# A two-layer mixture-of-experts behind a Fourier transform: where the second expert's token search stands in the program

## The chip, the cores and the metric

The kernel runs on one core of a Trainium2 chip. The metric is the device time of one execution in microseconds (us), smaller is better. Before the change it is 1285.11 us, the median of three runs (1282.51 to 1293.55).

A core has a matrix engine (TensorE, PE in the profile; the loads of its stationary operands are shown apart as PEld), a vector engine (VectorE, DVE), an activation engine (ScalarE, ACT), a general engine (GpSimd, POOL) and an engine that here only issues transfers (SyncE, SP). Each works through its own list of instructions in order and waits on semaphores for the others.

## What is computed

The input is transformed by the real part of a two-dimensional Fourier transform; its 9984 rows go through a first mixture-of-experts in which every expert takes exactly as many rows as its share, in the order of the logits, and the result goes through a second one with a plain arg-max.

```
X = fft(fft(x, axis=1), axis=2).real            # (4, 2496, 256) -> 9984 rows of 256

# first mixture: 8 experts, each takes cap = 9984 / 8 = 1248 rows
order = argsort(-(x @ w_gate).flatten())
for idx in order:                                # greedy, best logit first
    tok, e = idx // 8, idx % 8
    if assigned[tok] >= 0 or counts[e] >= cap: continue
    assigned[tok] = e; counts[e] += 1
for e in range(8):
    out[assigned == e] = relu(x[assigned == e] @ w1[e]) @ w2[e]

# second mixture, on the first one's output: e = argmax(x @ w_gate2),
# each row times its softmax weight and a sigmoid gate
```

## The kernel before

The program has three parts. `Fft` (to about 150 us of the span) does the transform with matrix products against tables (L305); its last loop, `rows` (L361), builds rows of the transformed input on VectorE, ScalarE and GpSimd and writes them to a buffer in memory (`xd<-xr`, L387). `Moe1` (to about 800 us) is the first mixture, `Moe2` the second.

The greedy assignment is not done row by row. `Select` (L443) runs eight *phases*. In each, the next expert to become full, and its 1248 rows, are found by a search for a threshold: eight *rounds* and a last count. A round is a loop between two engines: VectorE compares all logits with eight thresholds (L516), TensorE counts (ten small products, L521), VectorE folds the counts (L525 to L533), TensorE sums over the partitions (one product, L538; in the first phase L540), VectorE picks the new lower bound (L568, L573). Ahead of the rounds a phase prepares on VectorE (L548 to L562): the best logit of every row, which expert it belongs to, the steps of the search. Behind the last count it names the expert (`s_ei`, L598), takes its column out of the logits (L630) and numbers the chosen rows (to L633). I number phases, lists and experts from 0.

`places(k)` (L635) turns the numbers into a *list* of row indices: on VectorE L639 to L649 build one-hot factors `ha` and `hb`, TensorE multiplies them (four groups of ten products, L663, a `yield wait` ahead of the first), a second product (L673) and VectorE (L678 to L681) give `s_idx`. With the list GpSimd gathers the rows from `xd` (ten indirect transfers, L850).

`Moe1.ffn(k)` (L969) is the dense work of expert k in three chunks of rows: TensorE transposes the gathered rows (L867), ScalarE and VectorE split them in a high and a low half (L869, L870), TensorE makes the hidden layer (48 products a chunk, L801), ScalarE, VectorE and GpSimd split that (L881 to L887; the GpSimd share goes through three `hf` buffers that ScalarE writes, L884), and ten blocks of 24 products (L809) give the output, evacuated by ScalarE (L898). `route` (L901) then does the second mixture's gate for the expert's rows: some twenty small VectorE operations (L908 to L957), eleven products (L928, L930), two writes (L947, L948) and ten indirect scatters on GpSimd (L962). While the first expert waits for its rows, products on the weights that have already arrived keep TensorE at work (`busy`, L1011).

What stands where in the engines' lists is decided twice. `Flow` (L1115) holds a modelled clock: a unit of dense work moves it on by its length, and side generators (search, `prepare`, weights, gates, route, keep2) are advanced whenever their due time has come; what a generator yields is a delay, or a condition. Where the dense work cannot go on, `until` (L1160) advances the side work alone. The tile framework's scheduler then orders each engine's instructions out of what was emitted.

Before the change `Select.run` (L466) goes straight on from phase 0 and list 0 to phase 1, held only by `placed >= k - AHEAD`, which is true at once for k = 1. `Moe1.run` (L1083) starts the dense work of expert k when `ready >= k`, that is when list k, its gather, its first transposition and its weights have been emitted (`prepare`, L1018).

## Time and profile before

| | |
|---|---|
| runs | 1285.11, 1293.55, 1282.51 us |
| the profiled execution: its own time | 1291.67 us |
| its span, first to last instruction | 1289.9 us |
| TensorE busy | 1165.5 us, 90% of the span |
| VectorE / ScalarE / GpSimd busy | 57% / 35% / 39% |
| TensorE clock granted, mean share of full speed | 0.960 |

The profile's page gives busy times and the chain that ended last; the trace behind it can be asked for the instructions of a stretch in order of time. A row of that timeline has the start in us, the duration in us, engine, line, operation, the tile written and the tiles read, the shapes, how many were merged (x10), and in brackets how long the engine stood idle before it and what ended that. A group "x10" of TensorE is timed from its first start to its last end. A granted clock of 1.00 is 2.4 GHz, 0.50 is 1.2 GHz.

### The profile page before, as it was taken

How to read it: one execution, taken by the hardware profiler on the slowest of the kernel's cores; microseconds unless marked ns; L12 is line 12 of the kernel's file. 1: busy time of each engine (PE TensorE's matmuls, PEld its weight loads, DVE VectorE, ACT ScalarE, POOL GpSimd, SP SyncE). 2: the span in 40 equal slices, each digit the busy share in tenths (PEclk: the TensorE clock that was granted, in tenths of full speed). 3: DMA queues.
4: the chain of work that ended last, by engine and by line, in shares of the span. 5: the costliest groups of instructions: out<-in, count | busy, mean ns of one | idle time of the engine just before them, and what ended most of it. 6: DMA issues, size and time to landing. Idle time of an engine off the chain costs nothing. (4 is left out here: it accounts for less than half of the span.)

```text
span 1289.9 us, 25053 instructions
## 1 busy us (share of the span) xinstructions
PE 1165.5 (90%) x9998; PEld 837.6 (65%) x9998; DVE 733.8 (57%) x1885; ACT 447.7 (35%) x960; POOL 506.4 (39%) x495
## 2 busy tenths in 40 slices
PE   7999789878979969889896999799999999989998
PEld 4654456655646637557583756467576799878887
DVE  5867869784858857886562574443433333333333
ACT  3422344353523723535352443122322222222221
POOL 4723343475372660531505034524332333333321
PEclk8999789999899979999997999899999999999999
DMA  7835513131230651574846458443534266678782
GB/s 272 329 108 187 180 54 111 61 106 41 99 81 34 157 136 50 109 251 137 245 138 166 144 155 294 121 167 119 177 111 168 103 239 240 238 287 299 271 322 97
DMA packets 80040, 212.95 MB, mean 165 GB/s; under 512 B 11851, under 2 KB 48987, under 8 KB 69169
## 3 DMA queue, kind: packets, MB, share of 16 engines
q1 hardware_dynamic: 65360, 180.42, 41.9%
q0 software_dynamic: 14560, 30.91, 8.0%
q8 instruction: 79, 1.29, 0.4%
q14 instruction: 41, 0.33, 0.1%
HBM read 162.17 MB, written 50.42 MB: 165 GB/s over the span
## 5 line engine op out<-in xcount | busy, mean ns | idle before, releaser
L809 PEld LDWEIGHTS <-ht 128*128 128x128 f16 (+1 forms) x3912 | 383.5, 100 | 100.7 <-issue 26.2
L809 PE MATMUL py<-wh,ht 128*128 128x272 f16 (+2 forms) x3264 | 407.4, 281 | 25.4 <-issue 14.8
L801 PE MATMUL ph<-xt,wh 128*128 128x384 f16 (+4 forms) x2352 | 392.3, 318 | 7.2 <-DVE ht L887 4.0
L801 PEld LDWEIGHTS <-wh 128*128 128x128 f16 x2352 | 212.2, 100 | 128.6 <-issue 18.6
L1340 ACT ACTIVATE ht<-ph 128x512 f16<-128x512 f32 x166 | 97.9, 597 | 339.8 <-PE ph L801 269.3
L1341 DVE SCALAR_TENSOR_TENSOR ht<-ph,ht 128x512 f16<-128x512 f32 x166 | 113.7, 690 | 132.5 <-ACT ht L1340 118.7
L962 POOL DMA_INDIRECT lst<-r_en,r_pi x80 | 83.9, 1049 | 167.6 <-DVE r_pi L956 98.1
L881 ACT ACTIVATE ht<-ph 128x384 f16<-128x384 f32 (+1 forms) x192 | 98.4, 515 | 104.5 <-PE ph L801 89.3
L1353 POOL DMA_INDIRECT out<-ot,tarow x54 | 54.4, 1007 | 167.5 <-DVE ot L1352 156.4
L887 DVE SCALAR_TENSOR_TENSOR ht<-ph,ht 128x384 f16<-128x384 f32 (+1 forms) x147 | 85.0, 583 | 24.1 <-ACT ht L881 20.6
L850 POOL DMA_INDIRECT xg<-xd,s_idx x80 | 83.6, 1045 | 33.1 <-issue 23.2
L898 ACT ACTIVATE yr<-py 128x272 f32<-128x272 f32 x80 | 31.6, 395 | 173.1 <-PE py L809 121.3
L885 POOL TENSOR_TENSOR ht<-hf,ht 128x384 f16<-128x384 f32 (+1 forms) x45 | 48.3, 1076 | 88.9 <-ACT hf L884 82.1
L305 PE MATMUL big<-y,tab 128*128 128x36 f16 (+3 forms) x660 | 80.8, 274 | 1.2 <-DVE y L256 1.2
L809 PE MATMUL py<-wp,ht 128*128 128x256 f16 x648 | 75.9, 276 | 5.2 <-ACT ht L1340 3.9
L801 PE MATMUL ph<-xt,wp 128*128 128x256 f16 (+2 forms) x624 | 75.1, 279 | 3.8 <-DVE ht L1341 2.4
L1353 POOL DMA_INDIRECT out<-ot,tbrow x29 | 28.9, 995 | 116.1 <-DVE ot L1352 108.5
L1352 DVE TENSOR_SCALAR ot<-py,g 128x256 f32<-128x256 f32 x45 | 21.7, 483 | 83.9 <-PE py L809 71.5
L801 PEld LDWEIGHTS <-wp 128*128 128x128 f16 x624 | 51.5, 98 | 25.0 <-issue 7.7
L1077 DVE SCALAR_TENSOR_TENSOR wp<-g,wp 128x1024 f16<-128x1024 f32 x32 | 39.1, 1227 | 42.9 <-ACT wp L1076 33.3
L305 PEld LDWEIGHTS <-tab 128*128 128x128 f16 x660 | 38.7, 97 | 29.9 <-issue 2.7
L1352 DVE TENSOR_SCALAR ot<-py,xg 128x256 f32<-128x256 f32 x38 | 18.3, 483 | 64.7 <-PE py L809 57.1
(250 smaller groups left out, 1398.7 us busy)
## 6 DMA issues: line engine op xcount, KB each, us to landing
wh<-wsd SPq DMA_DIRECT2D x50, 1024.0 KB
wp<-wsd SPq DMA_DIRECT2D x26, 1024.0 KB
wf<-moe_w SPq DMA_DIRECT2D x32, 512.0 KB
g<-moe_w SPq DMA_DIRECT2D x32, 512.0 KB
wsd<-wp SPq DMA_DIRECT2D x32, 512.0 KB
xa<-xa SPq DMA_DIRECT2D x8, 1280.0 KB
xd<-xr SPq DMA_DIRECT2D x20, 512.0 KB
yd<-yr SPq DMA_DIRECT2D x8, 1156.5 KB
```

The source lines that it names most:

```text
L305: self.nc.tensor.matmul(dst, self.tabs[par][k][:, cs, c, u], self.y[par][:, cs, w, c, bs, qs], start=(n == 0), stop=(n == 3 * NCH - 1))
L801: Flow.pe = nc.tensor.matmul(dst, w1[:, dk, a, fk * 128:fk * 128 + 128], xt[:, b, dk, :n], start=(k == 0), stop=(k == 5))
L809: Flow.pe = nc.tensor.matmul(dst, ht[:, a, fk, t0:t0 + m], w2[:, fk // 4, b, fk % 4], start=(fk == 0 and a == 0 and b == 0), stop=(fk == 7 ...
L850: nc.gpsimd.indirect_dma_start(out=xg[:m, t], out_offset=None, in_=self.xd, in_offset=bass.IndirectOffsetOnAxis(ap=idx[:m, t:t + 1], axis=0))
L881: self.act = nc.scalar.activation(ht[:, 0, fk, :n], ph[:, :n], AF.Relu)
L885: nc.gpsimd.tensor_sub(ht[:, 1, fk, :n], hf[:, :n], ht[:, 0, fk, :n])
L887: nc.vector.scalar_tensor_tensor(ht[:, 1, fk, :n], ph[:, :n], 0.0, ht[:, 0, fk, :n], op0=OP.max, op1=OP.subtract)
L962: s = nc.gpsimd.indirect_dma_start(out=ent, in_=en[:m, t], in_offset=None, out_offset=bass.IndirectOffsetOnAxis(ap=pi[:m, t:t + 1], axis=0))
L1340: nc.scalar.activation(hi, src, AF.Relu)
L1341: nc.vector.scalar_tensor_tensor(lo, src, 0.0, hi, op0=OP.max, op1=OP.subtract)
L1352: nc.vector.tensor_scalar(ot, py[:, :D], g[:, h, D:D + 1], 2.0 ** -10, op0=OP.mult, op1=OP.mult)
L1353: st = nc.gpsimd.indirect_dma_start(out=self.out, in_=ot, in_offset=None, out_offset=bass.IndirectOffsetOnAxis(ap=row[:, 1, u + h:u + h + ...
```

## The change

Four edits. (1) `Select.run` waits ahead of phase 1 until `begun` is set; `Moe1.run` sets it at the point where the first expert's dense work begins to be emitted. (2) The preparation of phase 1 on VectorE (L548 to L562) is tied behind the last VectorE operation of list 0 (L681) by `issue_after`. (3) The modelled delay ahead of the first matrix products of list 0 becomes 7.0 instead of 6.0; the lists of the other experts keep 6.0. (4) The reduction that writes a list is kept under a name, for (2). What is computed stays the same.

```diff
@@ -394,6 +394,7 @@
 AHEAD = 3
+FIRST = 7.0
@@ -462,17 +463,24 @@
         self.placed = self.chosen = -1
+        self.begun = False
 
     def run(self):
 
         yield from self.start()
         for k in range(8):
             yield lambda: self.placed >= k - AHEAD
+            if k == 1:
+                yield lambda: self.begun
             yield from self.phase(k)
...
+    def behind(self, k):
+
+        return self.tc.issue_after(self.listed.ins) if k == 1 else ExitStack()
@@ -544,23 +552,24 @@
     def phase(self, k):
...
-        vm = w.tile([128, 80], F32, name="vm")
-        nc.vector.tensor_reduce(vm, self.lm, axis=AX.X, op=OP.max)
...
+        with self.behind(k):
+            vm = w.tile([128, 80], F32, name="vm")
+            nc.vector.tensor_reduce(vm, self.lm, axis=AX.X, op=OP.max)
...
@@ -647,7 +656,7 @@
-        wait = 6.0
+        wait = 6.0 if k else FIRST
@@ -678,7 +687,7 @@
-            nc.vector.tensor_reduce(self.idx[k], nf.rearrange("p g t -> p t g"), axis=AX.X, op=OP.add)
+            self.listed = nc.vector.tensor_reduce(self.idx[k], nf.rearrange("p g t -> p t g"), axis=AX.X, op=OP.add)
@@ -1108,6 +1117,7 @@
             flow.until(lambda: self.ready >= k and self.routed >= k - 2)
             self.at = k
+            self.sel.begun = True
             self.ffn(k, flow)
```

Line numbers rise by up to ten in the changed file: L548 there is L557, L639 is L648, L521 is L529, L538 is L546, L801 is L810, L809 is L818, L850 is L859, L867 is L876, L885 is L894, L928 and L930 are L937 and L939, L962 is L971.

Three places of the built program, as each engine's list has them. First VectorE at list 0, before; `vm`, `oe`, `ax`, `s_oh` belong to the preparation of phase 1, `u`, `pos`, `pi` to the list:

```order
L630 TENSOR_TENSOR lm<-lm,pen 128x640
L548 TENSOR_REDUCE vm<-lm 128x80
L553 TENSOR_TENSOR oe<-lm,vm 128x640
L613 CAST ct<-px 80x2
L554 TENSOR_TENSOR oe<-oe,s_w_94 128x640
L556 TENSOR_REDUCE ax<-oe 128x80
L621 SCALAR_TENSOR_TENSOR u<-px,gm,mm_1788 128x80
L622 TENSOR_TENSOR u<-px,mm_1788 128x80
L557 TENSOR_TENSOR s_oh<-s_w_94,ax 128x640
L623 TENSOR_TENSOR u<-u 128x80
```

The same place now:

```order
L639 TENSOR_TENSOR lm<-lm,pen 128x640
L622 CAST ct<-px 80x2
L630 SCALAR_TENSOR_TENSOR u<-px,gm,mm_1788 128x80
L631 TENSOR_TENSOR u<-px,mm_1788 128x80
L632 TENSOR_TENSOR u<-u 128x80
L634 SCALAR_TENSOR_TENSOR u<-u,mm_1788 128x80
L636 SCALAR_TENSOR_TENSOR s_alive<-u,s_alive 128x80
L640 TENSOR_SCALAR u<-u 128x80
L642 TENSOR_TENSOR pos<-u 128x80
L648 CAST pi<-pos 128x80
L353 SCALAR_TENSOR_TENSOR xg_1866<-big,xf 128x512
L649 TENSOR_SCALAR pi<-pi 128x80
```

The preparation of phase 1 and its first comparison (L516) have left this stretch; they stand behind the list (from L690, formerly L681), among the last rows of the transform and the first weights. On TensorE the first ten products of the list stand behind 35 products of the transform of 384 columns instead of 42.

Second, TensorE where expert 0 ends and expert 1 begins, before. The last rows of L809 are expert 0's last output block, L801 is expert 1's first hidden product; expert 1's first transpositions (L867) stand some blocks earlier:

```order
L809 MATMUL py<-wh,ht 96x272
L538 LDWEIGHTS ch
L538 MATMUL sp<-rd,ch 128x16
L786 LDWEIGHTS wt
...
L801 LDWEIGHTS wh
L801 MATMUL ph<-xt,wh 128x384
```

Now (L818 is the last block, L529 and L546 are rounds of phase 2, L937 and L939 the eleven products of expert 0's route, L876 the first transpositions of expert 1):

```order
L818 MATMUL py<-wh,ht 96x272
L546 LDWEIGHTS ch
L546 MATMUL sp<-rd,ch 128x64
L529 LDWEIGHTS s_oh
...
L937 MATMUL pt<-r_o_3405,ch 128x80
...
L939 MATMUL pt<-r_o_3405,ch 128x88
L546 LDWEIGHTS ch
L546 MATMUL sp<-rd,ch 128x64
L529 LDWEIGHTS s_oh
...
L876 MATMUL pt<-cf,xg 128x128 x3
L546 LDWEIGHTS ch
L546 MATMUL sp<-rd,ch 128x64
L810 LDWEIGHTS wh
L810 MATMUL ph<-xt,wh 128x384
```

Between the last output product of expert 0 and the first hidden product of expert 1 there now stand two and a half rounds of phase 2, expert 0's route and expert 1's first transpositions, and no dense work. The last product of list 1 (L673) is followed by only 38 output products of expert 0.

Third, GpSimd from expert 0's last hidden rows to expert 1's first, before:

```order
L885 TENSOR_TENSOR ht<-hf,ht 128x480 x2
L777 TENSOR_TENSOR wt<-wf,wt 128x256
L850 DMA xg<-xd,s_idx_85 128x256 x7
L885 TENSOR_TENSOR ht<-hf,ht 128x480
L850 DMA xg<-xd,s_idx_85 128x256 x2
L850 DMA xg<-xd,s_idx_85 96x256
L777 TENSOR_TENSOR wt<-wf,wt 128x256 x5
L885 TENSOR_TENSOR ht<-hf,ht 128x384 x2
```

And now:

```order
L894 TENSOR_TENSOR ht<-hf,ht 128x480 x3
L786 TENSOR_TENSOR wt<-wf,wt 128x256
L859 DMA xg<-xd,s_idx_85 128x256 x9
L859 DMA xg<-xd,s_idx_85 96x256
L786 TENSOR_TENSOR wt<-wf,wt 128x256
L971 DMA lst<-r_en,r_pi 81920x2 x10
L894 TENSOR_TENSOR ht<-hf,ht 128x384
```

Expert 0's ten scatters now stand in one piece ahead of the first hidden rows of expert 1, where they were spread among them and behind them.

## Rows read from the trace of the kernel before

**Rows 1.** The page, busy time of the engines: us (share of the span), instructions.

```profile
PE 1165.5 (90%) x9998; PEld 837.6 (65%) x9998; DVE 733.8 (57%) x1885; ACT 447.7 (35%) x960; POOL 506.4 (39%) x495
```

**Rows 2.** Table by stretch; the first line names the columns after the stretch.

```profile
core 0: us, PE busy (x) PEld busy (x) DVE busy (x) ACT busy (x) POOL busy (x), PEclk, DMA share, GB/s
...
137.70:145.20 7.50, 7.50 (x53) 5.31 (x53) 3.15 (x5) 0.00 (x0) 0.00 (x0) 0.54 0.57 188
...
249.60:275.00 25.40, 17.99 (x157) 11.62 (x157) 25.18 (x74) 17.34 (x43) 13.84 (x14) 1.00 0.33 110
```

**Rows 3.** Timeline of TensorE at list 0.

```profile
125.62 8.12 PE L305 MATMUL big<-y,tab 128*128 128x512 f16 x47
...
137.68 1.02 PE L663 MATMUL px<-ha,hb 128*128 128x40 f16 x10 [3.94 <-DVE ha L649]
...
140.00 3.06 PE L305 MATMUL big<-y,tab 128*128 128x384 f16 x9
```

**Rows 4.** Timeline of VectorE ahead of list 0's products.

```profile
123.67 0.82 DVE L548 TENSOR_REDUCE vm<-lm 128x80 f32<-128x640 f32 x1
124.53 0.82 DVE L553 TENSOR_TENSOR oe<-lm,vm 128x640 f16<-128x640 f32 x1
...
125.38 0.49 DVE L554 TENSOR_TENSOR oe<-oe,s_w 128x640 f16<-128x640 f16 x1
125.91 0.82 DVE L556 TENSOR_REDUCE ax<-oe 128x80 f16<-128x640 f16 x1
...
127.00 0.81 DVE L557 TENSOR_TENSOR s_oh<-s_w,ax 128x640 f16<-128x640 f16 x1
...
130.09 0.81 DVE L558 TENSOR_TENSOR s_vv<-vm,s_alive 128x80 f32<-128x80 f32 x1
...
131.51 1.34 DVE L516 SCALAR_TENSOR_TENSOR s_msk<-s_vv,s_lo,s_jw 128x640 f16<-128x640 f32 x1
...
134.09 0.76 DVE L641 TENSOR_SCALAR pi<-pi 128x80 int32<-128x80 int32 x1
134.78 0.19 DVE L643 CAST pa<-pi 128x80 f16<-128x80 int32 x1
```

**Rows 5.** Timeline of GpSimd: the last of eight additions of the transform's rows there.

```profile
134.08 0.71 POOL L378 TENSOR_TENSOR xr<-xg,xg 128x256 f32<-128x256 f32 x1
```

**Rows 6.** Timeline of GpSimd, then TensorE: first gather and first product of expert 0.

```profile
159.45 1.47 POOL L850 DMA_INDIRECT xg<-xd,s_idx  x1 [3.74 <-DMA xd<-xr]
...
165.74 0.33 PE L867 MATMUL pt<-cf,xg 128*128 128x128 f32 x1 [0.55 <-DMA xg<-xd,s_idx]
167.40 0.32 PE L801 MATMUL ph<-xt,wh 128*128 128x384 f16 x1 [1.33 <-ACT xt L869]
```

**Rows 7.** Timeline of TensorE, expert 0's first chunk: a round of phase 1.

```profile
174.88 0.20 PE L538 MATMUL sp<-rd,ch 64*128 64x64 f16 x1 [1.68 <-DVE rd L533]
```

**Rows 8.** Timeline: list 1's products, its first gather, last block of expert 0.

```profile
209.76 1.02 PE L663 MATMUL px<-ha,hb 128*128 128x40 f16 x10
...
220.44 0.96 POOL L850 DMA_INDIRECT xg<-xd,s_idx  x1 [4.53 <-DVE zs L573]
...
247.93 1.59 PE L809 MATMUL py<-wh,ht 128*96 128x272 f16 x12
...
249.88 2.44 PE L801 MATMUL ph<-xt,wh 128*128 128x384 f16 x14
```

**Rows 9.** Timeline: a round of phase 2 on TensorE, one operation of expert 0's route.

```profile
239.97 0.50 PE L521 MATMUL sp<-s_msk,s_oh 128*64 128x64 f16 x10
...
241.35 0.20 PE L538 MATMUL sp<-rd,ch 64*128 64x64 f16 x1
...
243.50 0.50 PE L521 MATMUL sp<-s_msk,s_oh 128*64 128x64 f16 x10
...
249.99 0.23 DVE L908 TENSOR_REDUCE r_mx<-yr 128x10 f32<-128x80 f32 x1
```

**Rows 10.** The page, costliest groups: busy us, mean ns of one, idle before.

```profile
L962 POOL DMA_INDIRECT lst<-r_en,r_pi x80 | 83.9, 1049 | 167.6 <-DVE r_pi L956 98.1
```

More of the change, by code (lines that the diff above doesn't have):

```diff
@@ L546, in phase @@
         f, h = self.f, self.h
-        vm = w.tile([128, 80], F32, name="vm")
-        nc.vector.tensor_reduce(vm, self.lm, axis=AX.X, op=OP.max)
-        sh = [128, 80, 8]
-        wt = self.w16[:, None, :].to_broadcast(sh)
-        oe = w.tile(sh, F16, name="oe", bufs=1)
-        nc.vector.tensor_tensor(oe, self.lm, vm[:, :, None].to_broadcast(sh), op=OP.is_equal)
-        nc.vector.tensor_mul(oe, oe, wt)
-        ax = w.tile([128, 80], F16, name="ax")
-        nc.vector.tensor_reduce(ax, oe, axis=AX.X, op=OP.max)
-        nc.vector.tensor_tensor(self.oh, wt, ax[:, :, None].to_broadcast(sh), op=OP.is_equal)
-        nc.vector.tensor_add(self.vv, vm, self.alive)
-        wd = w.tile([128, 1], F32, name="wd")
-        nc.vector.tensor_sub(wd, self.hi, self.lo0)
-        nc.vector.tensor_scalar(self.wr, f["pw"], wd, None, op0=OP.mult)
-        nc.vector.tensor_mul(self.jw, f["jt"][:, None, :].to_broadcast([128, ROUNDS, T]),
-                             self.wr[:, :, None].to_broadcast([128, ROUNDS, T]))
+        with self.behind(k):
+            vm = w.tile([128, 80], F32, name="vm")
+            nc.vector.tensor_reduce(vm, self.lm, axis=AX.X, op=OP.max)
+            sh = [128, 80, 8]
+            wt = self.w16[:, None, :].to_broadcast(sh)
+            oe = w.tile(sh, F16, name="oe", bufs=1)
+            nc.vector.tensor_tensor(oe, self.lm, vm[:, :, None].to_broadcast(sh), op=OP.is_equal)
+            nc.vector.tensor_mul(oe, oe, wt)
+            ax = w.tile([128, 80], F16, name="ax")
+            nc.vector.tensor_reduce(ax, oe, axis=AX.X, op=OP.max)
+            nc.vector.tensor_tensor(self.oh, wt, ax[:, :, None].to_broadcast(sh), op=OP.is_equal)
+            nc.vector.tensor_add(self.vv, vm, self.alive)
+            wd = w.tile([128, 1], F32, name="wd")
+            nc.vector.tensor_sub(wd, self.hi, self.lo0)
+            nc.vector.tensor_scalar(self.wr, f["pw"], wd, None, op0=OP.mult)
+            nc.vector.tensor_mul(self.jw, f["jt"][:, None, :].to_broadcast([128, ROUNDS, T]),
+                                 self.wr[:, :, None].to_broadcast([128, ROUNDS, T]))
         lo = self.lo0
```

## The prediction

> **What bounds the kernel now.** I read the page first: TensorE is busy for 1165.5 us of the span, 90% [rows 1]. So a change gains only where it takes away time in which TensorE stands still or runs at its low clock, and it loses where it makes such time. I therefore looked in the timeline for TensorE's idle times in the part that the change touches, from the end of the transform to the end of expert 1.
>
> Three things are to be seen. First, at list 0: TensorE ends its products of the transform at 133.74 (125.62 + 8.12) and then stands for 3.94 us until VectorE has `ha` for the list [rows 3]. VectorE is late because it does phase 1's preparation in between: seven operations of that phase stand ahead of or among those of the list, 0.82 + 0.82 + 0.49 + 0.82 + 0.81 + 0.81 + 1.34 = 5.91 us [rows 4]. The idle time has an aftermath: in the 7.5 us behind it the granted clock is 0.54, close to the lower level of 1.2 GHz [rows 2]. Second, the gather of expert 0 does not wait for the list. Its first transfer waits for the last write of the transform's rows, and starts at 159.45; the first product of expert 0 comes at 167.40, 7.95 us later [rows 6]. So list 0 matters only as it delays TensorE's way through the end of the transform, which ends in those writes. Third, between expert 0 and expert 1 nothing is waited for: the last block starts at 247.93 and runs 1.59, the first product of expert 1 follows at 249.88, and its gather had begun at 220.44, 29 us ahead [rows 8]. That lead is what the change spends.
>
> **The change, part by part.**
>
> *List 0 earlier (edits 2 and 3).* The 5.91 us leave VectorE's path to the list, so `ha` is no longer what TensorE waits 3.94 us for, or not for so long. The bounds: TensorE now comes to the list seven products sooner (35 instead of 42 of them ahead), at 8.12 / 47 = 0.17 us each 1.2 us sooner [rows 3], and VectorE up to 5.9 us sooner, so that the wait could vanish. But VectorE's small operations now meet GpSimd's eight additions, which end at 134.79 [rows 5]: beside them a small operation takes 0.76, without them 0.19 [rows 4]. Four of them (L640 to L644) at 0.57 more is 2.3 us of the 5.9 given back, which leaves 3.94 + 1.2 - 3.6 = 1.5 us of wait. I take that end, since the additions are where they were: 2.4 us are gained; the range is 0 to 3.9.
>
> *The clock behind it.* About 16 products of the transform in that stretch go at 3.06 / 9 = 0.34 instead of 0.17 us [rows 3]: 2.7 us. The list's own products lose nothing: ten take 1.02 at the low clock and 1.02 at the full one [rows 3, 8]. I take 2.5 us gained, because I expect that 1.5 us of idle time leave the clock up; if not, 0. The Trainium skill (TensorE: Matmul & The Clock Gate, Terms) counts the penalty as the low-clock time times the share of pulses left out. By that it would be 7.5 x 0.46 = 3.4 us, and the sum below 0.9 lower; no run here settles between the two yet, and I keep the rows' number.
>
> Together TensorE is at the end of the transform, the last writes out, the gather begun and expert 0 started 4.9 us earlier. The work that follows the transform's last products (its rows on VectorE) is as long as before: the preparation and three counts change places there.
>
> *Phase 1 inside expert 0 (edit 1).* All eight rounds of phase 1 now lie in expert 0; three of them lay ahead. They are moved, not added: phase by phase the same products are done. In the first chunk the wait of 1.68 us for a round [rows 7] goes, since the first round now stands behind 24 products. List 1 comes late in expert 0, tightly behind the phase; I allow 0.7 us for new waits there (0 to 2). Expert 0: -1.0.
>
> *The border of experts 0 and 1.* Phase 1 is three rounds later against the dense work, and so are list 1 and its gather. Only 38 output products follow the last product of list 1; at 1.59 / 12 = 0.13 us they last 5.0 us [rows 8]. The gather needs 7.95 us from its first transfer to the first product [rows 6], so at least 3 us are left bare. What decides, though, is TensorE's own list, which is in order: two and a half rounds of phase 2 stand ahead of expert 1's first transposition and product, with nothing to fill them. From counts to sum (L521 to L538) a round takes 1.38 us, from there to the next counts 2.15 [rows 9]. From the last output product: 0.9 (the rest of a round whose counts start just before it) + 2.15 + 1.38 + 2.15, then the counts' 0.43, and from the transposition to the first product 1.66 [rows 6]: 8.7 us. Expert 0's route shares VectorE with these rounds, some 20 operations of about 0.2 [rows 9]; if all were in the way it would be 4 us more, but much fits in VectorE's own waits. I take 9.5, in the range 5 to 12.7. In it lies moved work, two and a half rounds and the route's products, 1.8 us, which is missed elsewhere. Bare: +7.7 (3 to 11).
>
> *Its aftermath.* An idle time longer than that at list 0 will have the same low clock behind it, and the first chunk of expert 1 pays up to the 2.5 us of above. Part of the low clock falls into the idle time: +1.5 (0 to 2.7).
>
> *Expert 1.* Its first 25.4 us are VectorE's now: 25.18 busy, TensorE only 17.99, so 7.4 us of TensorE are lost there [rows 2], to phase 2's end, expert 0's route and the hidden layer at once. The route moves into the idle time at the border and phase 2's end to a later chunk, which takes most of that loss: -5.0. Four more rounds come into expert 1; they are moved work, but may each bring some tenths of waiting: +1.0. Expert 1: -4.0 (-7 to +2). From the end of expert 1 on the engines' lists are nearly the same as before, so I carry the difference to the end.
>
> **Sum.** -2.4 - 2.5 - 1.0 + 7.7 + 1.5 - 4.0 = -0.7 us. Against the profiled execution's 1291.67 that is 1291.0. That execution lies 6.6 above the median of the three runs (1285.11), so I forecast the median at 1285.11 - 0.7, rounded to 1284 us. The kernel's runs differ among themselves by 11 us; a change of less than 1% (12.9 us) is about what a measurement of it can not tell from none.
>
> **Rivals.**
>
> *The gain at the start stays and the border costs little* (faster). If phase 2's rounds at the border take only the time of the gather (3 us bare) and the clock stays up, the sum is -2.4 - 2.5 - 1.0 + 3 - 4.0 = -6.9: 1278 us. For it speaks that VectorE has no hidden layer to do there; against it that the loop of rows 9 was measured beside nearly idle VectorE already.
>
> *GpSimd becomes the bound at the border* (slower). Expert 0's ten scatters now stand ahead of the first hidden rows of expert 1 on GpSimd, behind ten gathers: 20 x 1.05 = 21 us at least [rows 10]. The hidden rows that go through GpSimd have three buffers, and the fourth is written by ScalarE in the second chunk, some 10 to 14 us after expert 1's start. If the twenty transfers end later than that (each has an issue gap, and VectorE's rounds run beside them), ScalarE stops, the hidden products' PSUM buffers fill, and TensorE stops too. It decides from the point where the scatters end more than about 14 us after the first product; each us beyond is a us lost. With 6 us of that, and the route's operations fully in the way (+3): -0.7 + 9 = +8: 1293 us. Against it: the gathers start some 12 us before expert 1 does.
> The Trainium skill (SBUF — State Buffer, Who interferes with whom) says that VectorE and GpSimd share one port pair as an exclusive lock, so that descriptors for an indirect transfer wait for a VectorE operation that holds it. By that rule this rival is stronger than the mean duration tells. Rows 4 and 5 agree with such blocking for additions; for the scatters no row here shows it.
>
> *The start brings nothing*: the gather is held by the writes' own transfer time and not by TensorE, so the 4.9 us are lost again ahead of expert 0, and the rest stays: +4.2: 1289 us. Against it: transfers are not the bound in that stretch, their engines' share is 0.57 [rows 2].
>
> **How the numbers follow.** The forecast (sum between -5 and +3) gets 0.5, the first rival 0.2, the second 0.2, the third 0.1. The ends of all terms at once lie far apart, but they do not come together; the range 1274 to 1294 takes in the three rivals and the spread of a median of three runs, and leaves out 2 in 10. All four cases lie within 1% of 1285. Only if the first rival comes with all terms at their good end is it faster by over 1%: 0.08. Slower by over 1% needs the second rival at twice its price: 0.06. That leaves 0.86 for within 1%.
>
> **What the profile afterwards would show.** Right: the wait ahead of list 0's first products is below 2 us, the stretch behind it has a clock near 1.00, the first gather starts near 154.5 and expert 0's first product near 162.5. Between the last output product of expert 0 and the first hidden product of expert 1 there are 8 to 11 us with only counts, route and transpositions on TensorE, and the granted clock falls around it. Expert 1's first 25 us have less than 4 us of idle TensorE. Wrong: if the wait at list 0 stays near 4 us, the first step fails; if the border is short, the loop of the rounds was not what holds it; if ScalarE waits for GpSimd in expert 1, the second rival holds. A time outside 1274 to 1294 would mean that the difference does not stay in this stretch, which is where I have looked.

## The result, and the profile after

The changed kernel takes 1301.1 us, the kernel before 1284.76 (medians of 20 runs each, in turn): a ratio of 1.0127, interval 1.0104 to 1.0150. It is slower by 16 us. I had forecast 1284 within 1274 to 1294, and had given "slower by over 1%" a chance of 0.06.

The profiled executions differ by about the same amount, 17.1 us (1289.9 and 1307.0 us of span). I cut both at the first hidden product of each expert (L801, now L810):

| us | before | after | difference | forecast |
|---|---|---|---|---|
| start of expert 0 | 167.40 | 160.49 | -6.9 | -4.9 |
| expert 0 with the border | 82.5 | 88.0 | +5.5 | +6.7 |
| expert 1 | 84.9 | 103.6 | +18.7 | -2.5 |
| from expert 2 to the end | 955.1 | 954.9 | -0.2 | 0 |

So three of the four lines came as forecast or near it, and one, expert 1, is the whole miss. The page shows hardly anything of that: TensorE is busy 8.5 us longer than in [rows 1], for the same number of products.

```profile
PE 1174.0 (90%) x9998; PEld 841.0 (64%) x9998; DVE 739.2 (57%) x1885; ACT 450.3 (34%) x960; POOL 512.8 (39%) x495
```

The table by stretch, with the columns of [rows 2], shows where: the stretch behind list 0's first products, the border, expert 1's first 25.4 us and its rest.

```profile
130.35:137.85 7.50, 7.49 (x59) 5.66 (x59) 4.85 (x7) 2.05 (x8) 4.49 (x4) 0.77 0.29 96
...
238.00:248.49 10.49, 3.42 (x37) 2.61 (x38) 5.55 (x30) 0.70 (x2) 6.83 (x8) 0.52 0.35 110
248.49:273.89 25.40, 20.35 (x152) 11.61 (x152) 15.06 (x51) 10.45 (x28) 13.78 (x16) 0.86 0.14 37
273.89:352.06 78.17, 63.56 (x552) 43.41 (x551) 59.93 (x163) 29.64 (x73) 36.16 (x33) 0.89 0.21 71
```

Expert 1's first 25 us have 5.1 us of idle TensorE (25.40 - 20.35) where [rows 2] had 7.4. The change did take something away there, though 2.3 us and not the 5.0 that I had counted on. But the granted clock in expert 1 is 0.86 and 0.89; it was 1.00 in [rows 2] and in the whole of expert 1 before. In the clock's own records 24.0 us of expert 1 now lie at the lower level and 0.0 before; the idle times over 0.3 us add up to 19.3 us, 13.3 before. What TensorE waited for in expert 1 (us in total, times, longest):

```profile
PE sp L546 <- DVE rd L541: 6.6, 1, 6.6
PE sp L529 <- DVE s_msk L524: 3.9, 2, 3.2
PE pt L876 <- DVE wh L802: 3.5, 1, 3.5
PE pt L876 <- DVE xt L879: 2.0, 1, 2.0
```

The longest, 6.6 us, looks like a wait for VectorE, but the timeline of that stretch (start, duration, in brackets the idle time ahead and what ended it) shows another thing. TensorE's last products start at 312.66 and stop; VectorE, which needs the count of 312.23, stands for 6.81 us and is released at 319.44 with TensorE's completion, just when the row of ten gathers on GpSimd has landed:

```profile
312.23 0.50 PE L529 MATMUL sp<-s_msk,s_oh 128*64 128x64 f16 x10
312.66 0.98 PE L810 MATMUL ph<-xt,wh 128*128 128x480 f16 x4
...
316.94 0.93 POOL L859 DMA_INDIRECT xg<-xd,s_idx  x1 [0.30 <-issue]
...
319.44 0.22 DVE L533 TENSOR_TENSOR dm<-sp,cf 64x64 f32<-64x64 f32 x1 [6.81 <-remote]
...
320.26 0.23 PE L546 MATMUL sp<-rd,ch 64*128 64x64 f16 x1 [6.62 <-DVE rd L541]
```

I call this a late completion: the semaphore update of a product is recorded microseconds behind the product's recorded end. (The profile models that end, so it can't tell whether the product itself or only its update came late.) Up to 860 us the profile of the kernel before has 15 of them over 1.5 us (updates within 0.5 us of each other taken as one; the longest 11.5), the changed one 20, nearly all beside indirect transfers of GpSimd. It was my first suspect.

### The profile page after: what moved, and what is told of

The parts are those of the page before. It is cut to its first block, busy times and chain, and to the rows that moved or that the text cites. A ratio compares the mean times of both kernels' runs of the same rounds, so it can differ in the third digit from the quotient of the medians.

```text
span 1307.0 us, 25060 instructions
## 1 busy us (share of the span) xinstructions
PE 1174.0 (90%) x9998; PEld 841.0 (64%) x9998; DVE 739.2 (57%) x1885; ACT 450.3 (34%) x960; POOL 512.8 (39%) x495
## 5 line engine op out<-in xcount | busy, mean ns | idle before, releaser
L818 PEld LDWEIGHTS <-ht 128*128 128x128 f16 (+1 forms) x3912 | 386.2, 101 | 107.8 <-issue 31.4
L818 PE MATMUL py<-wh,ht 128*128 128x272 f16 (+2 forms) x3264 | 414.9, 284 | 31.9 <-issue 21.0
L810 PE MATMUL ph<-xt,wh 128*128 128x384 f16 (+4 forms) x2352 | 395.0, 321 | 10.8 <-DVE ht L896 9.7
L810 PEld LDWEIGHTS <-wh 128*128 128x128 f16 x2352 | 213.2, 100 | 137.4 <-issue 28.2
L971 POOL DMA_INDIRECT lst<-r_en,r_pi x80 | 83.4, 1043 | 176.6 <-DVE r_pi L965 101.9
L859 POOL DMA_INDIRECT xg<-xd,s_idx x80 | 82.9, 1037 | 40.1 <-issue 21.9
L894 POOL TENSOR_TENSOR ht<-hf,ht 128x384 f16<-128x384 f32 (+1 forms) x45 | 46.1, 1025 | 96.6 <-ACT hf L893 84.0
L818 PE MATMUL py<-wp,ht 128*128 128x256 f16 x648 | 74.5, 273 | 3.8 <-ACT ht L1350 2.5
L810 PE MATMUL ph<-xt,wp 128*128 128x256 f16 (+2 forms) x624 | 73.0, 277 | 0.0
L810 PEld LDWEIGHTS <-wp 128*128 128x128 f16 x624 | 51.6, 98 | 19.1
L305 PEld LDWEIGHTS <-tab 128*128 128x128 f16 x660 | 38.5, 97 | 29.3 <-issue 2.0
```

Of the source, the lines that this page charges most:

```text
L305: self.nc.tensor.matmul(dst, self.tabs[par][k][:, cs, c, u], self.y[par][:, cs, w, c, bs, qs], start=(n == 0), stop=(n == 3 * NCH - 1))
L810: Flow.pe = nc.tensor.matmul(dst, w1[:, dk, a, fk * 128:fk * 128 + 128], xt[:, b, dk, :n], start=(k == 0), stop=(k == 5))
L818: Flow.pe = nc.tensor.matmul(dst, ht[:, a, fk, t0:t0 + m], w2[:, fk // 4, b, fk % 4], start=(fk == 0 and a == 0 and b == 0), stop=(fk == 7 ...
L859: nc.gpsimd.indirect_dma_start(out=xg[:m, t], out_offset=None, in_=self.xd, in_offset=bass.IndirectOffsetOnAxis(ap=idx[:m, t:t + 1], axis=0))
L894: nc.gpsimd.tensor_sub(ht[:, 1, fk, :n], hf[:, :n], ht[:, 0, fk, :n])
L971: s = nc.gpsimd.indirect_dma_start(out=ent, in_=en[:m, t], in_offset=None, out_offset=bass.IndirectOffsetOnAxis(ap=pi[:m, t:t + 1], axis=0))
```

## The experiments

All kernels compute the same as the kernel before. There were sixteen runs, in four groups of four. The kernels of a group ran beside each other and shared the runs of the kernel before, so a ratio holds within its group. The groups fell on two levels: the kernel before took 1304.4 and 1285.6 us in groups 1 and 3 and 1227.8 and 1227.6 in groups 2 and 4. Groups 1 and 2 ran on the same chip, so the level doesn't go with the chip. In groups 1 and 3 every profile has 13 to 19 late completions over 1.5 us up to 860 us, in groups 2 and 4 none has one. The stages, cut as above, in us; a round of the search is counted where its sum (L538 before, L546 in the changed kernel) stands, a phase's last count included:

| run (group) | ratio to before, interval | expert 0 starts | expert 0 | expert 1 | experts 2 to 4 | rounds in expert 1 |
|---|---|---|---|---|---|---|
| e1_spread (1) | 1.0099, 1.0060 to 1.0138 | 160.7 | 88.2 | 101.4 | 261.5 | 13 |
| e2_tie_alone (1) | 1.0005, 0.9969 to 1.0041 | 162.3 | 88.4 | 90.7 | 255.0 | 10 |
| e3_wait_alone (1) | 1.0101, 1.0056 to 1.0147 | 166.2 | 92.9 | 102.6 | 249.7 | 13 |
| e4_row (1) | 1.0011, 0.9979 to 1.0043 | 163.7 | 83.7 | 92.2 | 263.3 | 9 |
| b2_before (2) | (one run) | 163.7 | 78.0 | 80.1 | 236.4 | 9 |
| e8_gates (2) | 1.0148, 1.0124 to 1.0171 | 159.5 | 83.0 | 95.1 | 243.4 | 12 |
| e7_phase3_later (2) | 1.0198, 1.0167 to 1.0229 | 160.2 | 82.9 | 83.3 | 259.3 | 10 |
| e9_gates_late (2) | 1.0117, 1.0094 to 1.0140 | 164.8 | 79.8 | 98.7 | 237.9 | 12 |
| a2_after (3) | 1.0146, 1.0107 to 1.0186 | 161.2 | 87.6 | 102.7 | 251.6 | 13 |
| e2b_tie_alone (3) | 1.0026, 0.9993 to 1.0059 | 165.8 | 83.7 | 90.6 | 248.0 | 10 |
| e5_phase2_later (3) | 1.0092, 1.0054 to 1.0130 | 166.6 | 78.9 | 88.9 | 267.6 | 12 |
| e10_faster (3) | 1.0122, 1.0082 to 1.0163 | 159.0 | 89.0 | 111.6 | 240.6 | 16 |
| b3_before (4) | (one run) | 164.0 | 78.0 | 80.1 | 235.2 | 9 |
| a3_after (4) | 1.0103, 1.0066 to 1.0140 | 161.1 | 83.0 | 92.7 | 240.4 | 13 |
| e11_spaced (4) | 1.0102, 1.0070 to 1.0133 | 162.9 | 83.3 | 91.8 | 238.8 | 13 |
| e7b_phase3_later (4) | 1.0238, 1.0205 to 1.0272 | 160.8 | 83.4 | 84.4 | 260.8 | 10 |

### Group 1: which edit, and is it the row of scatters?

Theory A: the twenty indirect transfers in a row at the border (ten gathers, then ten scatters) make the loss, by late completions. Theory B: the search, which comes later, makes it.

**e1_spread** puts expert 0's scatters behind operations of expert 1 on GpSimd; nothing else moves.

```diff
-                nc.gpsimd.tensor_sub(ht[:, 1, fk, :n], hf[:, :n], ht[:, 0, fk, :n])
+                self.low = nc.gpsimd.tensor_sub(ht[:, 1, fk, :n], hf[:, :n], ht[:, 0, fk, :n])
...
+        if k == 0:
+            yield lambda: self.at > 0
+            yield 5.0
         for t in range(10):
-            s = nc.gpsimd.indirect_dma_start(...)
+            with self.tc.issue_after(self.low.ins) if k == 0 else ExitStack():
+                s = nc.gpsimd.indirect_dma_start(...)
```

> The changed kernel, with expert 0's ten scatters spread over expert 1 (each tied behind a GpSimd operation of expert 1's hidden layer); the lists of the other engines are the same, row for row. In the changed kernel expert 1 takes 103.6 us (248.49 to 352.06) against 84.9 before (249.88 to 334.77), and the completions of TensorE's products come up to 3 us late beside the ten gathers and ten scatters that GpSimd issues in a row at 231 to 259. Theory A, the row of transfers makes the loss: expert 1 takes 90 to 95 us, no late completion over 1.5 us stands at 247 to 262, and the kernel is 7 to 12 us faster than the changed one, a ratio to the kernel before of 1.003 to 1.007. Theory B, the later search makes it (phase 2's end, its rounds and the hidden layer on VectorE at once): expert 1 stays at 101 to 105 us, ratio 1.011 to 1.015.

**e2_tie_alone** leaves out the wait for `begun`, **e3_wait_alone** has nothing but that wait, **e4_row** is the kernel before with expert 0's scatters in a row.

```diff
-            if k == 1:
-                yield lambda: self.begun
```

> The changed kernel without the wait for `begun`: the preparation of phase 1 still stands behind the first list on VectorE and the list's delay is still 7.0, but phase 1's rounds go straight on behind the list, as before. Both theories: the wait ahead of the list's products is as short as in the changed kernel (1.0 us, from 3.9), expert 0 starts 3 to 7 us earlier than before, experts 0 and 1 take what they took before (82.5 and 84.9, 3 us either way), so the kernel is 3 to 7 us faster than before, ratio 0.994 to 0.998. If the gain at the start is lost again ahead of expert 0, the ratio is 0.999 to 1.002.

> The kernel before with the wait for `begun` alone; the preparation of phase 1 isn't tied and the list's delay is 6.0. In its VectorE list the preparation stands ahead of the list's operations again. If the tie makes the gain at the start: the wait ahead of the list's products is 3.5 to 4.5 us, expert 0 starts 3 to 5 us later than in the changed kernel (160.5), and the kernel is slower than the changed one: ratio to the kernel before 1.013 to 1.018. If the wait for `begun` alone gives the gain at the start: expert 0 starts at 159 to 162 and the ratio is 1.010 to 1.014. Expert 1 takes 100 to 106 us under both theories of the loss.

```diff
-            yield 2.0 if k == 6 else 8.0 if k == 7 else 4.0
+            yield 0.0 if k == 0 else 2.0 if k == 6 else 8.0 if k == 7 else 4.0
```

> The kernel before with expert 0's ten scatters emitted at once (delay 0 between them instead of 4.0): they stand in rows of four and six on GpSimd, where they stood in rows of one to three among the operations of expert 1's hidden layer; the search is where it was. Theory A, the row of transfers makes the loss: expert 1 takes 89 to 97 us instead of 84.9, late completions of TensorE of more than 2 us stand beside the rows, ratio 1.003 to 1.009. Theory B: expert 1 takes 83 to 87 us, ratio 0.998 to 1.002.

A fell as far as the scatters go, by the times of the whole kernel. Spread, they leave expert 1 at 101.4, inside what B wanted for it, and the ratio at 1.0099, a little under what B wanted; in rows of four and six in the kernel before they cost 0.1%, within its interval. There expert 1 alone, at 92.2, lies in A's range (89 to 97), with one completion 5.0 us late in it, so the stage speaks for late completions where the whole doesn't. The wait for `begun` alone brings the loss, 1.0101. The tie alone brings no gain, 1.0005, though I had expected one of 3 to 7 us under both theories. Its timeline of TensorE shows one reason: phase 1's rounds stand ahead of expert 0 with their preparation still to come, and TensorE waits for them twice, 2.65 and 3.28 us. (The third wait is for a weight.)

```profile
144.27 0.69 PE L527 MATMUL sp<-s_msk,s_oh 128*64 128x64 f16 x10 [2.65 <-DVE s_msk L522]
148.25 0.23 PE L544 MATMUL sp<-rd,ch 64*128 64x64 f16 x1 [3.28 <-DVE rd L539]
150.99 7.22 PE L1023 MATMUL py<-wh 128*128 128x512 f16 x39 [2.51 <-ACT wh L763]
```

e3 gives the other half: without the tie expert 0 starts at 166.2, as in the kernel before. The tie alone starts it at 162.3, but then expert 0 takes 88.4.

### Group 2: late gate columns, or many rounds?

Phase 1 names expert 1 at 210 us instead of 199, so its weights come later, and with them the four groups of L795 that fold the second gate into them. In the kernel before these stood at 238.0, 249.6, 273.6 and 284.0, half of them ahead of expert 1; now at 254.2, 272.1, 282.0 and 292.5, all inside. Expert 1's output blocks are not emitted before the fourth (`gated >= k`), so side work is emitted alone meanwhile: expert 1 is 63.3 long in the emitter's modelled clock, 52.5 before. Theory C makes this the loss.

```diff
-            for d in self.W.gate(*self.gs.pop(k), self.wg, self.P["psum"], k in WG):
+            for d in self.W.gate(*self.gs.pop(k), self.wg, self.P["psum"], k in WG, 4.0 if k == 1 else GG):
```

(The new last argument is the delay ahead of each group. **e8_gates** is this on the changed kernel; **e9_gates_late** is the kernel before with 10.7 there; **e7_phase3_later** is the changed kernel with `yield 21.0` ahead of phase 3.)

> The kernel before, profiled once more beside the next three: expert 0 takes 80 to 89 us, expert 1 85 to 93. It gives the stages of these runs their own base.

> The changed kernel with expert 1's gate columns made sooner: the delay GG ahead of each of the four groups of L795 is 4.0 for expert 1 instead of 8.0. In the changed kernel phase 1 names expert 1 later (210 instead of 199 us), so its weights come later and all four groups stand inside expert 1 (254 to 292), where before two of them stood ahead of it (238, 249.6, then 274, 284). Where the emission of expert 1's output blocks waits for them, side work is emitted alone: expert 1 takes 63.3 in the emitter's modelled clock, 52.5 before, and 52.1 in this run. Theory C, the late gate columns make the loss: expert 1 takes 86 to 95 us, less time of it at the low clock, and the kernel is 7 to 12 us faster than the changed one, ratio to the kernel before 1.001 to 1.006. Theory B, 13 rounds of the search in expert 1 instead of 9 make it (there are 12 here): expert 1 stays at 98 to 105 us, ratio 1.009 to 1.014.

> The kernel before, with only the gate columns of expert 1 made later: the delay ahead of each of its four groups is 10.7 instead of 8.0, so that expert 1 takes as long in the emitter's modelled clock as in the changed kernel (63.3). Search phases 1 and 2, list 1 and the border of experts 0 and 1 stay where they were. Theory C: expert 1 gets 7 to 14 us longer than in the kernel before beside it, ratio 1.005 to 1.011. Theory B or the border: expert 1 gets at most 3 us longer, ratio 0.998 to 1.003.

> The changed kernel with a delay of 21.0 ahead of phase 3: expert 1 holds 9 counts of the search instead of 13, as few as before or fewer; the gate columns of expert 1 are as late as in the changed kernel. Theory B (the number of rounds): expert 1 takes 86 to 95 us, ratio to the kernel before 1.002 to 1.008, if experts 2 and 3 don't pay for the rounds that come to them. Theory C (the late gate columns): expert 1 stays at 97 to 105 us, ratio 1.009 to 1.014.

b2_before was faster than I had expected, on the faster level. Each theory got one yes. e9: late gate columns alone make expert 1 18.6 us longer than in b2_before and the kernel 1.2% slower. But they also make side work bunch up (12 rounds instead of 9), and 11.6 us are four waits for weights that GpSimd prepares, the longest behind a row of scatters; the changed kernel has next to none of these (0.4 us in a3_after), so a good part of e9's loss is another one:

```profile
285.45 0.93 POOL L962 DMA_INDIRECT lst<-r_en,r_pi  x1 [0.30 <-issue]
286.41 0.92 POOL L885 TENSOR_TENSOR ht<-hf,ht 128x384 f16<-128x384 f32 x1
...
287.79 1.29 POOL L777 TENSOR_TENSOR wt<-wf,wt 128x256 f16<-128x256 f32 x2
288.51 0.24 PE L786 MATMUL pt<-m_wg,wt 128*128 128x16 f16 x3 [6.38 <-POOL wt L777]
```

e7 has expert 1's gate columns as late as the changed kernel (the first three groups 5.7, 17.9 and 28.2 us behind its start, 5.8, 18.0 and 28.0 in a3_after; the fourth 31.7 and 38.5), and 10 rounds: expert 1 takes 83.3, only 3.2 more than b2_before. So late gate columns cost little where no rounds come due meanwhile. e8 failed as a cure: sooner, the gate products meet weights that are not there yet, and one wait of 9.8 us (for L795) replaces the stall; without it expert 1 would be at 85.3. And e7 as a whole is the slowest kernel yet, since experts 2 to 4 pay 23 us for what expert 1 saves.

### Group 3: lateness by itself

> The changed kernel once more, timed and profiled beside the next three and beside the second profile of the kernel before (b2_before: expert 0 starts at 163.7 and takes 78.0, expert 1 takes 80.1, expert 2 78.5; no completion of TensorE comes late there). If the late completions beside rows of transfers were the loss, it is gone here: expert 1 takes 80 to 85 us, ratio 0.998 to 1.005. If the later search makes it, expert 1 takes 90 to 97 us, and the ratio is 1.011 to 1.018. In both cases expert 0 starts at 159 to 161 and its dense work with the border takes 82 to 84 us.

> The changed kernel without the wait for `begun`, once more: the first run gave 1.0005 (0.9969 to 1.0041), too wide to tell a gain of 3 us from none. If the gain at the list reaches the end: expert 0 starts at 159 to 162 against 163.7, ratio 0.995 to 0.998. If it is lost again ahead of expert 0 or in it: ratio 0.999 to 1.003.

```diff
             yield lambda: self.placed >= k - AHEAD
+            if k == 2:
+                yield 21.0
```

That is **e5_phase2_later**, on the kernel before. **e10_faster** is the changed kernel with the delays of a round in phases 1 and 2 cut from 2.3 and 1.8 to 1.3 and 0.9.

> The kernel before with a delay of 21.0 ahead of phase 2 (as much as the change moves it in the emitter's modelled clock); list 0, phase 1, list 1, the gate columns and the weights of expert 1 stay where they were. If the later search by itself makes the loss: ratio 1.008 to 1.020, with the time lost in experts 1 and 2 (together 8 to 20 us more than the 158.6 of b2_before). If the border and the late weights of expert 1 make it: ratio 0.998 to 1.004.

> The changed kernel with a faster search in expert 0: the modelled delays of a round in phases 1 and 2 are 1.3 and 0.9 instead of 2.3 and 1.8, so that list 1 and phase 2 fit into expert 0 and its dense work no longer ends ahead of them (expert 1 begins at 125.1 in the modelled clock, as in the kernel before, instead of 135.7). If lateness of the search is the cost: the border has no bare rounds, expert 1 takes 80 to 88 us, and the kernel is 10 to 20 us faster than the changed one, ratio 0.996 to 1.004. If 20 rounds are too many for expert 0, it takes 86 us or more and the ratio stays at 1.005 to 1.015.

a2_after repeats the first profile within a microsecond in expert 1, late completions included, so it could not tell what the time is without them. e2b settles the tie: no gain (1.0026), with a start at 165.8. e5 shows that a later phase 2 costs 0.9% by itself, without `begun`, list 0 or the border touched. The time isn't lost in expert 1 (88.9) but in expert 2, 97.8 us against 83.8 in a2_after. Expert 2 is the one whose gate columns come late there: all four groups stand inside it (338.1 to 367.5), one of four in a2_after. And it shows that the number of rounds by itself is not what costs: expert 2 holds 12 rounds in e5, in a2_after and in b3_before, where it takes 97.8, 83.8 and 78.5. e10 went as its second outcome: expert 0 takes 89.0, and 16 rounds come to lie in expert 1, which takes 111.6.

### Group 4: with and without late completions

> The kernel before, profiled beside the next three: expert 1 takes 80 to 92 us, experts 0 and 1 together 158 to 174.

> The changed kernel beside them: expert 1 takes 102 to 104 us if TensorE's completions come late again beside the rows of transfers, and 87 to 95 if they don't (as in b2_before, e8_gates, e7_phase3_later and e9_gates_late, where none did). Ratio to the kernel before 1.011 to 1.017 if the rounds make the loss, whether completions come late or not; 1.003 to 1.008 without late completions if these make it.

**e11_spaced** is e1_spread with the gathers of expert 2 also tied one by one.

```diff
-                nc.gpsimd.indirect_dma_start(out=xg[:m, t], ...)
+                with self.tc.issue_after(self.low.ins) if k == 2 else ExitStack():
+                    nc.gpsimd.indirect_dma_start(out=xg[:m, t], ...)
...
-                yield 0.0 if t < 4 else GY
+                yield 3.0 if k == 2 else 0.0 if t < 4 else GY
```

> The changed kernel with the scatters of expert 0 and the gathers of expert 2 taken apart on GpSimd (each tied behind an operation of expert 1's hidden layer; rows of at most five are left); the rounds stay, 13 in expert 1. If the rows make the loss: at most one late completion over 2 us in expert 1, which takes 88 to 96 us, ratio 1.003 to 1.009. If the number of rounds makes it: expert 1 stays at 98 to 104 us, ratio 1.011 to 1.017.

> The changed kernel with a delay of 21.0 ahead of phase 3, once more (10 rounds in expert 1; the rows of ten stand as in the changed kernel). If the number of rounds makes the loss in expert 1: it takes 10 us or more less than in a3_after, and experts 2 to 4 take 15 us or more longer than there, as the rounds come to them. If the rows make it: expert 1 takes at most 4 us less than in a3_after.

This group settled the late completions. None comes in any of its profiles up to 860 us, and the changed kernel is slower all the same, 1.0103; taking the rows of transfers apart changes nothing, 1.0102. (e11's expert 1, 91.8, lies in the range that I had set for the rows, but with the rows in place it is 92.7, so it doesn't speak for them.) Late completions seem to add to the loss where they occur: expert 1 is 92.7 us without and 102.7 with them, and in the kernel before 80.1 and 84.9. They don't make it. With three rounds less, expert 1 falls to 84.4, which is B's outcome, 2 us short of the size that I had asked for; experts 2 to 4 get 20.4 us longer.

The pair b3_before and a3_after is the cleanest reading of expert 1. (As wholes the two profiles differ by 20.4 us, the medians of this group by 12.3, so the pair overstates the change as a whole.) First the two rows of the table by stretch for expert 1 (before, then changed; columns as in [rows 2]), then the costliest groups of TensorE in it (busy us, mean ns; idle before), before and changed:

```profile
241.97:322.07 80.10, 72.37 (x647) 50.78 (x644) 65.62 (x193) 38.66 (x97) 49.54 (x50) 0.96 0.31 87
...
L809 PE MATMUL py<-wh,ht 128*128 128x272 f16 (+1 forms) x240 | 32.8, 288 | 0.0
L801 PE MATMUL ph<-xt,wh 128*128 128x384 f16 (+1 forms) x144 | 30.0, 347 | 0.4 <-DVE ht L887 0.4
L521 PE MATMUL sp<-s_msk,s_oh 128*64 128x64 f16 (+1 forms) x100 | 5.1, 200 | 5.3 <-DVE s_msk L516 3.7 <-DVE s_hi L588 1.6
```

```profile
244.12:336.80 92.68, 80.67 (x701) 54.23 (x701) 78.86 (x214) 40.28 (x100) 53.38 (x54) 0.92 0.25 75
...
L818 PE MATMUL py<-wh,ht 128*128 128x272 f16 (+1 forms) x240 | 35.6, 303 | 0.0
L810 PE MATMUL ph<-xt,wh 128*128 128x384 f16 (+1 forms) x145 | 31.3, 353 | 0.3 <-ACT xt L878 0.3
L529 PE MATMUL sp<-s_msk,s_oh 128*64 128x64 f16 (+1 forms) x140 | 7.3, 199 | 4.8 <-DVE s_msk L524 3.3 <-DVE s_hi L597 1.4
```

Of expert 1's 12.6 us, 4.3 are idle time (12.0 - 7.7). 4.1 are the same dense products at a lower clock (35.6 - 32.8 and 31.3 - 30.0; granted 0.92 instead of 0.96). The last 4.2 are other work that came in, 2.2 of it the counts.

The new idle time is mostly waiting for VectorE, and in the timeline one case shows how. A round's smallest operation, L541, takes 0.22 us at 306.07 and 2.89 at 309.28: three subtractions on GpSimd, which had queued up behind the row of gathers, run one after the other beside it, and TensorE waits 2.57 us for the sum.

```profile
306.07 0.22 DVE L541 TENSOR_TENSOR rd<-s_bs,r 64x64 f16<-64x64 f16 x1
...
308.87 3.20 POOL L894 TENSOR_TENSOR ht<-hf,ht 128x480 f16<-128x480 f32 x3
...
309.28 2.89 DVE L541 TENSOR_TENSOR rd<-s_bs,r 64x64 f16<-64x64 f16 x1
...
312.23 0.20 PE L546 MATMUL sp<-rd,ch 64*128 64x64 f16 x1 [2.57 <-DVE rd L541]
```

What the bunching does to TensorE's list can be counted. Between a round's counts and its sum there stand, in expert 1 of b3_before, 24, 6, 15, 7, 9, 6, 18, 23 and 22 dense products, in order. In a3_after it is 5, 3, 8 and 8 at its beginning (the end of phase 2) and 19, 8, 7, 4, 4, 5, 7, 7 and 11 further on. Between a sum and the next counts it is, apart from two long stretches in each, 11 to 17 in b3_before and 8 to 17 in a3_after. At 0.24 us each, four products of 480 columns are 0.98 us, less than the 1.38 that the loop needs from counts to sum [rows 9]. Nothing is left in reserve, so each delay of VectorE, and each late completion, is an idle time of TensorE, and some have a low clock behind them. In e5_phase2_later expert 2 shows the same pattern (12, 12, 12, 19, 8, 7, 4, 4, 4, 7, 7, 7), and there the time is lost in expert 2; with as many rounds a2_after has 25, 4, 11, 11, 12, 12, 12, 12, 6, 22, 12 and 24 there, and 14.0 us less.

No version of these beats the kernel before; e2 and e4 are level with it.

## Why the prediction was wrong, step by step

**List 0 earlier: right.** The wait is 1.02 us, 2.9 less than in [rows 3]; I had taken 2.4. The preparation left VectorE's path, and two of its small operations still take 0.77 beside GpSimd, as in [rows 4]. The clock behind it is 0.77 instead of 0.54, so about half of the 2.5 us came back. The start of expert 0 over all profiles lies at 159.0 to 162.9 with both edits and at 163.7 to 167.4 with the kernel before and those that share its start (e3 to e5, e9). By the means the gain is 3.2 us on the faster level and 5.6 on the slower, forecast 4.9; the profile of [rows 6] was at the late end.

**The border: right in kind.** From the last output product (234.71 + 0.66) to expert 1's first product (248.49) TensorE has only counts, sums, the route and transpositions. It is 13.1 us, outside my 5 to 12.7, because one wait in it, behind late completions, takes 5.72; in a3_after the same wait is 1.66 and the border 7.8 (236.33 to 244.12). Expert 0 with the border came out at +5.5 and +5.0 (88.0 - 82.5, 83.0 - 78.0), forecast +6.7. In the first pair that nearness is in part luck: the border is 12.8 us longer (0.36 before) and the rest of expert 0 7.2 us shorter, where I had put +9.5 and, with the moved work, -2.8. In the other pair it is +7.4 and -2.4.

```profile
234.71 0.66 PE L818 MATMUL py<-wh,ht 128*96 128x272 f16 x4
...
246.33 0.75 PE L529 MATMUL sp<-s_msk,s_oh 128*64 128x64 f16 x10 [5.72 <-DVE s_msk L524]
...
248.49 0.80 PE L810 MATMUL ph<-xt,wh 128*128 128x384 f16 x2 [0.33 <-ACT xt L878]
```

The same place in a3_after:

```profile
235.66 0.67 PE L818 MATMUL py<-wh,ht 128*96 128x272 f16 x4
...
241.97 0.74 PE L529 MATMUL sp<-s_msk,s_oh 128*64 128x64 f16 x10 [1.66 <-DVE s_msk L524]
...
244.12 1.11 PE L810 MATMUL ph<-xt,wh 128*128 128x384 f16 x3 [0.26 <-ACT xt L878]
```

**Expert 1: the step that failed.** The route was to take "most of that loss: -5.0", and: "Four more rounds come into expert 1; they are moved work, but may each bring some tenths of waiting: +1.0." With the clock's +1.5 that was -2.5; it measured +12.6 where no completion came late and +18.7 where they did. Three things were wrong in it.

First, moved work is free only if it leaves time that was worth something. Two and a half of the rounds lay ahead of expert 0, in time in which TensorE has nothing but products on weights that have already arrived to pass the time. The timeline of TensorE in b3_before shows them there. In a3_after the place is simply empty:

```profile
148.81 0.20 PE L538 MATMUL sp<-rd,ch 64*128 64x64 f16 x1 [1.86 <-DVE rd L533]
150.78 0.74 PE L521 MATMUL sp<-s_msk,s_oh 128*64 128x64 f16 x10 [1.78 <-DVE s_msk L516]
152.42 0.23 PE L538 MATMUL sp<-rd,ch 64*128 64x64 f16 x1 [0.89 <-DVE rd L533]
152.58 8.20 PE L1016 MATMUL py<-wh 128*128 128x512 f16 x39
```

```profile
148.34 7.65 PE L1025 MATMUL py<-wh 128*128 128x512 f16 x39 [5.27 <-ACT wh L765]
```

I had called them moved, not added, as if their place made no difference. There they cost next to nothing: TensorE then waits for the gather, and e3, which has them moved and little else, starts expert 0 no sooner (166.2) than kernels that have them there (163.7 to 167.4).

Second, I did not follow what else hangs on phase 1. It names the expert, the name starts the weights, the weights the gate columns, and these hold the emission of the output blocks. I read the order of the built program at the border, but not the distance between rounds inside expert 1, where it could have been counted before any run.

Third, beyond the +1.5 for its first chunk I left the clock out of expert 1. In the profile before it had 13.3 us of idle time and no low clock ([rows 2] shows 1.00), and I took that as given. That was a lucky profile: in b3_before expert 1 has 7.6 us of idle time and 6.8 us at the lower level. With 6 us more idle time, 24 us of it are at the lower level in the changed kernel. The dense products of expert 1 (before, then changed; busy us, mean ns) show the price:

```profile
L809 PE MATMUL py<-wh,ht 128*128 128x272 f16 (+1 forms) x240 | 31.3, 279 | 2.7 <-DVE wh L793 1.5 <-issue 1.2
L801 PE MATMUL ph<-xt,wh 128*128 128x384 f16 (+1 forms) x144 | 29.2, 340 | 1.7 <-DVE ht L887 1.7
```

```profile
L810 PE MATMUL ph<-xt,wh 128*128 128x384 f16 (+1 forms) x145 | 36.0, 391 | 2.2 <-DVE ht L896 1.8 <-ACT xt L878 0.3
L818 PE MATMUL py<-wh,ht 128*128 128x272 f16 (+1 forms) x240 | 34.2, 294 | 0.0
```

So of the 18.7 us of the first pair, 9.7 are the same products at a lower clock, 5.5 more idle time (19.65 - 14.19) and 3.5 other work: the clock is the largest part, and I had put +1.5.

**After expert 1: right in the first pair.** The difference at expert 2's start, 17.3 us, is the difference at the end, 17.1. Between b3_before and a3_after it grows from 14.7 to 20.4, so that this too held for one pair only.

**The rivals.** *The gain stays and the border costs little* did not come; nor did *the start brings nothing* (the gather starts at 152.36, was 159.45). *GpSimd becomes the bound* had the right sign and the wrong mechanism: ScalarE waits for GpSimd in expert 1 not at all in the first profile and 0.9 us in a3_after, and with the scatters spread (e1, e11) the time stays. GpSimd does matter, by holding VectorE in a3_after and by late weights in e9. What the runs point to, a later search whose rounds bunch up where late gate columns hold back the output blocks, was none of my rivals: I had it as a term of +1.0.

**What stays open.** How the 12.6 us divide between the rounds' spacing, the late gate columns and the phase's end was not measured apart; e7b and e5 change them together. The number by itself is ruled out only by expert 2, which with 12 rounds takes 83.8 us in a2_after and 97.8 in e5. That the spacing turns delays into idle time is read from the order and the waits, not tried by itself.

## What to carry over

Before counting moved work as neutral, look at what TensorE does in the time that it leaves: here side work in a forced wait was nearly free, and the same work between dense products cost its own time, the waits of its loop and the low clock behind these. When a chain starts later, follow everything that hangs on it to the next place where the emitter or an engine waits for all of it, and count there how many products stand between the steps of a loop. This change saved 3 to 6 us at the start of expert 0 and cost 13 to 19 in expert 1.

## What the runs showed of the hardware

The same program ran on two levels, 1228 and 1285 to 1304 us. The slower one goes with late completions of TensorE's products, up to 13.4 us (in e2_tie_alone), nearly always beside indirect transfers on GpSimd; on the faster level there is not one over 1.5 us up to 860 us in eight profiles. Both levels came on the same chip (groups 1 and 2). Taking a row apart did not reliably end them (in e1_spread a row of five had one of 3.5 us). What holds them was not found, nor whether they make the slower level or only go with it.

A VectorE operation can stand behind several GpSimd operations in a row, not only one. In e7_phase3_later an operation of 0.24 us takes 8.19, until six subtractions on GpSimd are over, and TensorE waits 11.34 us for the count behind it:

```profile
354.85 8.19 DVE L636 SCALAR_TENSOR_TENSOR u<-u,mm 128x80 f32<-128x80 f32 x1
...
356.24 6.69 POOL L772 TENSOR_TENSOR wh<-wf,wh 128x512 f16<-128x512 f32 x6
...
365.20 0.69 PE L531 MATMUL sp<-s_msk,s_oh 128*64 128x64 f16 x10 [11.34 <-DVE s_msk L526]
```

The Trainium skill (SBUF — State Buffer, Who interferes with whom) says that only the port pair shared by VectorE and GpSimd contends, as an exclusive lock. The trace agrees, and the case above is its reverse direction to the one that I had cited: here GpSimd's arithmetic holds VectorE, for 8.19 us.
